# Attention with rotary embedding and an MLP on one core: the first four weight chunks move from GpSimd's DMA queue to SyncE's, and the planner's load rate and due times are new

## The chip, the core and the metric

The kernel runs on one core of a Trainium2 chip. The metric is the device time of one execution in microseconds; the median of several runs stands for a kernel. Five engines work side by side, each through its own list of instructions in order: TensorE (PE in the profile), VectorE (DVE), ScalarE (ACT), GpSimd (POOL) and SyncE (SP). Here SP and POOL hardly compute; they issue DMAs. What SP issues goes to one DMA queue (q1 in the profile), what POOL issues to another (q0), and 16 DMA engines serve both.

## The reference

Inputs are float32. There are 4 batches, 8 heads, 576 positions, 64 columns a head; the MLP is 512 to 2048 to 512 over all 2304 tokens.

```python
q_rot, k_rot = (rotate(q), rotate(k))            # [x1 cos - x2 sin, x1 sin + x2 cos]
scores = np.matmul(q_rot, k_rot.transpose(0, 1, 3, 2)) / np.sqrt(D)
attn = np.exp(scores - np.max(scores, axis=-1, keepdims=True))
attn = attn / (np.sum(attn, axis=-1, keepdims=True) + 1e-09)
x = np.matmul(attn, v)      # heads put side by side: 2304 x 512
h = x @ w_in
g = np.where(h >= 1, h, np.where(h <= -1, 0.0, (h + 1) ** 2 / 4))
out = g @ w_out
```

The rounding of the reference is kept by splitting each float32 operand into two float16 parts and adding three products of them (hi hi, hi lo, lo hi).

## The kernel before

**Data.** Heads are worked in four pairs j. For each batch and pair the host has laid out two copies of keys and queries, transposed: the plain one, and one with the halves of each head exchanged. A rotation (`turn`, L325) is then three products on DVE: first copy times cosines (L328), second copy times sines (L330), their sum (L332). The cosines and sines are the table `rt`. Queries come in two blocks of 256 columns (`hf` 0 and 1) and 64 left-over columns (`rqL`). For batch 0 every pair of block 0 has loads of its own (keys 288 KB a copy, queries 128 KB a copy), later ones are merged.

**Splits.** `prep_k`, `load_q`, `prep_left` and `load_v` issue the loads of keys, queries, left-over columns and values. A factor from the sum of squares of the keys (ACT square L292, a small matmul L298, four small DVE steps) scales the split of keys and queries into high part (ACT L339) and low part (DVE L341).

**Attention.** `softmax_item` (L535) takes scores of a pair of heads for 128 rows: maximum on DVE (L543), exponent on ACT (L545), high part on ACT (L553), low part on DVE (L555). A DMA transpose on SP's queue (`dmaT`, L287) turns them into `pT`, and PE multiplies them with the values (L598).

**Weights.** There are 16 chunks of 1 MB, w_in and w_out by turns, i = 2c + which. `prep_w` (L481) loads one into a buffer that is free at that time: in the order `rawseq` the last regions of the weight store itself, then the value buffer `rv` and the second key buffer `kT[1]`. Chunks 0 to 3 go into four different regions, chunks 4 to 7 into the same four again, once the earlier ones are decoded. Chunk 14 goes into `kT[1]`, which nobody holds at the start. Decoding is three DVE steps (L493, L495, L497), then the high part on ACT (L506). For the first ten chunks the low part comes from PE: a product with the identity and one with a scaled diagonal (L522, L523) into the two banks `psO`, read by ACT (L526). The MLP (`mlp_block`, L661) uses the same banks `psO` for its second layer (L709), after those; its first layer is L679.

**The order.** Nothing runs in the order of the program text. Every step is given to `Plan.add` with an engine, a cost in ns, a place `at` and what it reads and writes. `wanted()` (L104) lays PE's steps one behind the other by `at`, from 18,000 ns on, and works a due time back from each step's users: minus its own cost and a lag, which for a DMA is 1300 ns and its bytes at the load rate (`bw`). `order()` (L123) adds a number from the table SLACK, by the group's name and by the name with its part ("raw k0.02 sp": loads of keys, batch 0, pair 2, on SP), and then runs through time: an engine that is free takes, of the steps that are ready, the one with the lowest sum. In this run a load moves over one shared wire at the load rate. What comes out is one list for each engine, which the chip then executes in that order, with waits only for what a step reads and writes.

Of the kernel before, what the change touches and what calls it, by code (L numbers as in the profile page):

```python
# [13 lines left out]
U32 = mybir.dt.uint32  # L14
# [8 lines left out]


SLACK = {
    "k0 dve": 41_100, "k0.00 dve": 46_400, "k1 act": 617_700, "k1 dve": 63_800, "k1.10 dve": 21_800,
    "k1.12 dve": 13_200, "k1.20 act": 39_400, "k1.20 dve": -4_900, "k1.30 dve": 385_800, "left0 act": -440_200,
    "left0 dve": -34_700, "left0.01 dve": 29_800, "left1 act": -682_100, "left1.20 dve": 4_500,
    "left1.22 dve": -1_000, "left1.32 pe": 57_700, "mlp0 act": -48_700, "mlp0 dve": -56_400, "mlp0 pe": 1_362_600,
    "mlp0.0.1 act": 186_100, "mlp0.0.2 act": 74_000, "mlp0.0.7 act": -87_400, "mlp1 dve": -637_500,  # L30
    "mlp1.1.2 act": -106_800, "mlp1.1.3 act": -122_000, "mlp2 act": -875_300, "mlp2 dve": 47_700,
    "mlp2 pe": 40_700, "mlp2.2.2 act": 1_200, "mlp2.2.3 pe": 45_800, "mlp2.2.4 dve": 63_100, "mlp3 act": -691_900,
    "mlp3 dve": -81_700, "mlp3 pe": -23_800, "mlp3.3.3 pe": 241_700, "mlp3.3.4 pe": 225_400,
    "mlp3.3.7 act": 43_400, "mlp3.3.7 pe": 162_900, "mlp3.4.2 pe": -800, "mlp3.5.1 pe": 65_600,
    "mlp3.5.2 dve": -202_300, "mlp3.5.2 pe": 29_400, "mlp3.5.7 pe": 34_500, "mlp3.6.1 pe": 20_600,
    "mlp3.6.2 pe": 25_500, "mlp3.6.7 pe": 163_600, "mlp3.7.0 pe": 82_200, "mlp3.7.3 pe": -15_800,
    "pv0 dve": -448_200, "pv0 pe": -769_100, "pv1 act": -1_444_600, "pv1 dve": -252_200, "pv1.123 pe": 71_100,
    "pv1.302 pe": -66_700, "q0 act": 100_000, "q0 dve": -18_900, "q0.001 act": -77_800, "q0.003 dve": 48_700,
    "q0.010 dve": 109_300, "q0.012 dve": 36_700, "q1 dve": 44_500, "q1.100 dve": -20_700, "q1.110 dve": 8_500,
    "q1.200 dve": -37_600, "q1.210 act": 52_900, "ql0 dve": -134_800, "ql1 dve": 190_900, "raw k0 sp": -12_600,  # L40
    "raw k0.00 sp": -14_800, "raw k0.01 sp": -368_000, "raw k0.02 sp": -12_000, "raw k0.03 sp": 11_100,
    "raw k1 sp": -1_486_700, "raw q0 sp": -6_000, "raw q0.000 sp": -9_500, "raw q0.002 sp": 50_400,
    "raw q0.003 sp": 221_800, "raw v0.0 sp": 71_700, "raw w.1 pool": -67_500, "s0 act": -70_500,
    "s0 dve": -190_500, "s0.001 dve": -66_100, "s0.003 dve": -18_000, "s0.021 dve": 65_100, "s0.022 act": 55_200,
    "s0.022 sp": 21_200, "s0.023 act": 27_000, "s0.031 act": -118_200, "s1 dve": -166_700, "s1 pe": -550_500,
    "s1.101 act": -14_300, "s1.102 act": -34_500, "s1.110 dve": -25_600, "s1.111 dve": -17_400,
    "s1.112 dve": -6_800, "s1.121 dve": 40_400, "s1.122 act": -77_600, "s1.123 act": -123_500,
    "s1.123 dve": 215_800, "s1.132 act": -109_900, "s1.201 dve": -42_600, "s1.202 dve": -25_800,
    "s1.202 sp": 14_100, "s1.210 dve": -33_500, "s1.221 dve": 5_400, "s1.223 act": -71_400, "s1.232 act": -5_500,
    "s1.233 dve": 35_700, "s1.301 dve": -5_700, "s1.302 act": -166_600, "s1.303 dve": -11_800,  # L50
    "s1.312 sp": -17_900, "s1.320 dve": -4_400, "scale0.01 dve": 99_100, "v0 act": 59_900, "v0 dve": 80_400,
    "v1 act": -52_700, "v1.2 act": 119_900, "w act": -90_000, "w dve": 37_800, "w.5 dve": 7_600,
}


# [128 lines left out]
def kernel(  # L184
# [73 lines left out]
    plan = Plan()  # L258
    counts = {}

    def ring(name, n):
        c = counts.get(name, 0)
        counts[name] = c + 1
        return c % n
# [4 lines left out]
    def act_cost(n, psum=False, ptrs=1):  # L269
        return (51.0 if psum else 93.0) + 0.833 * n + 93.0 * ptrs  # L270

    def dve_cost(n, psum=False, ptrs=0):
        return (65.0 if psum else 69.0) + 1.042 * n + 61.0 * ptrs
# [6 lines left out]

    def dma(at, dst, src, r, w, nbytes, eng="sp"):
        q = nc.sync if eng == "sp" else nc.gpsimd
        plan.add(eng, 600.0 if eng == "sp" else 1000.0, at, lambda: q.dma_start(out=dst, in_=src), r, w, bw=nbytes / 300.0)

    def dmaT(at, dst, src, r, w, nbytes):
        plan.add("sp", nbytes / 221.0 + 60.0, at,
# [2 lines left out]
    def add_square(at, x, lo, np_, scr, scrkeys, col, colkey, srckeys):  # L289
        n = x.shape[-1]  # L290
        plan.add("act", act_cost(n), at,
                 lambda: nc.scalar.activation(out=scr[lo:lo + np_, 0:n], in_=x, func=AF.Square, accum_out=col),  # L292
                 r=srckeys, w=[colkey] + scrkeys)
# [187 lines left out]
    def prep_w(which, c, at):  # L481

        yi, i = ring("ybufs", 2), 2 * c + which
        (raw, rk_), y, yk = rawseq[i], ybufs[yi], ykeys[yi]
        plan.group, plan.part = "raw w", c
        dma(at, raw, (w_out if which else w_in).bitcast(U32)[c], [], rk_, 128 * 8192, "pool")
        plan.group = "w"
        words = raw.rearrange("p (n t) -> p n t", t=2)
        lw, hw = words[:, :, 0], words[:, :, 1]
        u = y.bitcast(U32)  # L490
        hi, lo = [ws[:, i, l] for l in range(2)]

        plan.add("dve", 602.0, at, lambda: nc.vector.tensor_scalar(  # L493
            out=u, in0=hw, scalar1=3, scalar2=0x3FFFFFFF, op0=ALU.logical_shift_left, op1=ALU.bitwise_and), r=rk_, w=yk)
        plan.add("dve", 1135.0, at, lambda: nc.vector.scalar_tensor_tensor(  # L495
            out=u, in0=lw, scalar=29, in1=u, op0=ALU.logical_shift_right, op1=ALU.bitwise_or), r=rk_ + yk, w=yk)
        plan.add("dve", 1135.0, at, lambda: nc.vector.scalar_tensor_tensor(  # L497
            out=u, in0=hw, scalar=0xC0000000, in1=u, op0=ALU.bitwise_and, op1=ALU.bitwise_or), r=rk_ + yk, w=yk)
        if c == 0:
            cols = [3 * which, 3 * which + 1]  # L500
            for e, j in enumerate(cols):
                add_square(at, y[:, 512 * e:512 * e + 512], 0, 128, r_s, ["r"], ssw[:, j:j + 1], ("ssw", j), yk)
            p, ri = root(at, ssw[:, 3 * which:3 * which + 3], [("ssw", 3 * which + j) for j in range(3)])
            wcol[which] = (times(at, p, 2.0 ** 64), times(at, ri, 2.0 ** (10 - 64)))
# [241 lines left out]
    at = 0.0  # L746
# [126 lines left out]
```

## Time and profile before

| | us |
|---|---|
| runs before, median of 3 (lowest, highest) | 635.91 (634.6, 638.42) |
| the profiled execution | 636.13 |
| its span in the trace | 634.4 |
| PE, DVE, ACT busy in the span | 559.6, 510.6, 441.5 |

A busy time is the time in which an engine had an instruction under way. It is best read by stretches, since the limit changes: the start with loads and preparation, a long middle part with attention of the batches beside the MLP of earlier blocks, and an end with the MLP alone. Matmuls are pipelined, so a busy PE is not PE at its peak. DMA issues are shown under SPq, and under POOL, at the time of their issue; how long data takes is read from the queues.

### The profile page before, as it was taken

To read this page: it belongs to the slowest core of one execution; us is meant where nothing else is said; L and a number is where in the kernel's file an instruction comes from. 1 tells how busy PE (TensorE), PEld (TensorE's weight loads), DVE (VectorE), ACT (ScalarE), POOL (GpSimd) and SP (SyncE) were. 2 spreads that over 40 slices of the span, in tenths; PEclk is the share of its full clock that TensorE was granted. 3 is DMA by queue.
4 is the path that set the end of the run, shared out by engine and by line. 5 is a ranking of instruction groups with operands and counts; after the bars stand their busy time and mean duration, and the time that the engine had idled before them with its cause. 6 is when DMAs were issued, how large, how long until landed. Compare 5 with 4: busy or idle time off the path is not lost.

```text
span 634.4 us, 12628 instructions
## 1 busy us (share of the span) xinstructions
PE 559.6 (88%) x5078; PEld 358.7 (57%) x5078; DVE 510.6 (80%) x839; ACT 441.5 (70%) x881; POOL 9.3 (1%) x22
## 2 busy tenths in 40 slices
PE   0146657999889899999999999999999999999996
PEld 0023223566565666665666666666666667666663
DVE  1999989999999899999899789968877684334332
ACT  1478768997989789998777799766777574223221
POOL 2000100000000000000000000000000000000000
PEclk9999788999999999999999999999999999999999
DMA  8997797828699968686668675666464664000000
GB/s 335 389 299 146 260 253 203 179 74 178 136 184 249 211 137 199 122 212 141 119 160 177 106 146 115 100 91 107 91 140 75 117 128 90 1 1 35 1 34 17
DMA packets 188009, 91.31 MB, mean 144 GB/s; under 512 B 170160, under 2 KB 178608, under 8 KB 185904
## 3 DMA queue, kind: packets, MB, share of 16 engines
q1 hardware_dynamic: 185648, 73.74, 55.7%
q0 software_dynamic: 2304, 16.78, 7.4%
q8 instruction: 39, 0.64, 0.4%
q14 instruction: 18, 0.15, 0.1%
HBM read 40.96 MB, written 4.72 MB: 72 GB/s over the span
## 4 chain that ended last, share of the span: by engine, by line
PE 54%; DVE 24%; DMA 11%; ACT 6%; issue 3%; SPq 0%; ACTq 0%; DVEq 0%
PE psO L709 20%; PE psH L679 20%; DMA pT<-phl 9%; PE psV L598 6%; DVE phl L555 5%; PE psS L569 5%; DVE mx L543 4%; ACT phl L553 2%; DMA rk<-in_km_dram 2%; ACT p L545 1%; PE psO L522 1%; DVE g L700 1%; PE psS L581 1%; DVE r L696 1%; DVE dup L330 1%
## 5 line engine op out<-in xcount | busy, mean ns | idle before, releaser
L709 PE MATMUL psO<-w,g 128*128 128x512 f16 x864 | 211.2, 380 | 1.2 <-ACT g L698 0.9
L679 PEld LDWEIGHTS <-w 128*128 128x128 f16 x1920 | 171.2, 98 | 48.2 <-issue 6.2
L679 PE MATMUL psH<-xT,w 128*128 128x256 f16 x1536 | 188.8, 273 | 3.2 <-ACT a L686 2.2
L555 DVE SCALAR_TENSOR_TENSOR phl<-p,sums,phl 128x576 f16<-128x576 f32 x144 | 113.4, 812 | 18.1 <-ACT phl L553 17.6
L553 ACT ACTIVATE phl<-p,sums 128x576 f16<-128x576 f32 x144 | 106.7, 766 | 30.6 <-DMA pT<-phl 17.3
L545 ACT ACTIVATE p<-psS,mx 128x576 f32<-128x576 f32 x144 | 105.4, 733 | 29.1 <-DVE mx L543 25.8
L709 PEld LDWEIGHTS <-g 128*128 128x128 f16 x864 | 78.8, 98 | 75.8 <-issue 3.2
L543 DVE TENSOR_REDUCE mx<-psS 128x1 f32<-128x576 f32 x144 | 103.8, 748 | 3.5 <-PE psS L569 2.2
L700 DVE SCALAR_TENSOR_TENSOR g<-r,g 128x512 f16<-128x512 f32 x72 | 49.4, 686 | 52.6 <-ACT g L698 51.5
L569 PE MATMUL psS<-kT,qT 64*128 64x512 f16 (+1 forms) x768 | 68.1, 300 | 19.5 <-ACT p L545 17.4
L686 ACT ACTIVATE a<-psH 128x512 f32<-128x512 f32 x72 | 42.4, 589 | 60.5 <-PE psH L679 60.1
L569 PEld LDWEIGHTS <-qT 64*128 64x128 f16 x768 | 32.5, 97 | 64.8 <-issue 43.4
L698 ACT ACTIVATE g<-r 128x512 f16<-128x512 f32 x72 | 44.9, 623 | 28.1 <-PE psO L709 17.1
L598 PE MATMUL psV<-pT,vS 128*64 128x256 f16 (+1 forms) x768 | 49.5, 251 | 4.1 <-DMA pT<-phl 4.1
L696 DVE SCALAR_TENSOR_TENSOR r<-a,r 128x512 f32<-128x512 f32 x72 | 49.5, 687 | 0.9
L689 DVE SCALAR_TENSOR_TENSOR r<-a 128x512 f32<-128x512 f32 x48 | 33.1, 689 | 19.7 <-ACT a L686 18.8
L598 PEld LDWEIGHTS <-vS 128*64 128x64 f16 x768 | 33.0, 111 | 16.0 <-issue 14.2
L298 PE MATMUL psV<-ssk,ones 128*128 128x1 f32 (+1 forms) x14 | 3.4, 314 | 29.3 <-ACT w L292 28.9
L598 PE MATMUL psV<-pT,vM 128*64 128x256 f16 (+1 forms) x480 | 28.5, 249 | 0.0
L545 ACT ACTIVATION_READ_ACCUMULATOR p<-psS,mx 128x1 f32 x144 | 28.0, 194 | 0.0
L679 PE MATMUL psH<-xL,w 128*128 128x128 f16 x384 | 26.2, 219 | 0.0
L598 PEld LDWEIGHTS <-vM 128*64 128x64 f16 x480 | 21.9, 112 | 0.1
(98 smaller groups left out, 476.7 us busy)
## 6 DMA issues: line engine op xcount, KB each, us to landing
w<-in_w_in_dram POOLq DMA_DIRECT2D x7, 1024.0 KB, 7.5
w<-in_w_out_dram POOLq DMA_DIRECT2D x6, 1024.0 KB, 7.9
rv<-in_vm_dram SPq DMA_DIRECT2D x8, 512.0 KB, 6.2
out_dram<-o SPq DMA_DIRECT2D x16, 256.0 KB, 2.4
rq<-in_qm_dram SPq DMA_DIRECT2D x7, 512.0 KB, 5.0
dup<-in_qm_dram SPq DMA_DIRECT2D x7, 512.0 KB, 4.0
rk<-in_km_dram SPq DMA_DIRECT2D x6, 576.0 KB, 5.1
dup<-in_km_dram SPq DMA_DIRECT2D x6, 576.0 KB, 5.4
```

What stands on the lines that cost most here:

```text
L543: plan.add("dve", dve_cost(S, psum=True), at, lambda m=m, src=src: nc.vector.tensor_reduce(out=m, in_=src, op=ALU.max, axis=AX.X, negate=T ...
L545: plan.add("act", act_cost(S, psum=True, ptrs=2), at, lambda a=a, e=e, m=m, src=src: nc.scalar.activation(out=p32[e], in_=src, func=AF.Exp ...
L553: plan.add("act", act_cost(S), at, lambda a=a, e=e, hi=hi: nc.scalar.activation(out=hi, in_=p32[e], func=AF.Copy, scale=rr[:, a:a + 1]), r ...
L555: plan.add("dve", dve_cost(S, ptrs=1), at, lambda a=a, e=e, hi=hi, lo=lo: nc.vector.scalar_tensor_tensor(out=lo, in0=p32[e], scalar=rr[:, ...
L569: nc.tensor.matmul(out=psS[a][:, lo:hi], lhsT=qT[hf][d, l, j, c:c + 128], rhs=kT[ks][d, j, m, lo:hi], start=z == 0, stop=z == 2)
L598: nc.tensor.matmul(out=outs[a], lhsT=st, rhs=moving(a, blk), start=z == 0, stop=z == len(seq) - 1)
L679: nc.tensor.matmul(out=psH[:, n * i:n * i + n], lhsT=wi[ft // 2][:, wl, kk, 128 * (ft % 2):128 * (ft % 2) + 128], rhs=xfn(xl, kk), start=z ...
L686: plan.add("act", act_cost(512, psum=True, ptrs=0), at, lambda one=one: nc.scalar.activation(out=a, in_=psH, func=AF.Relu, scale=2.0 ** -7 ...
L696: plan.add("dve", dve_cost(512), at, lambda one=one: nc.vector.scalar_tensor_tensor(out=r, in0=a, scalar=one, in1=r, op0=ALU.max, op1=ALU. ...
L698: plan.add("act", act_cost(512, ptrs=0), at, lambda g=g, one=one: nc.scalar.activation(out=g[:, 0], in_=r, func=AF.Relu, scale=1.0, bias=- ...
L700: plan.add("dve", dve_cost(512), at, lambda g=g, one=one: nc.vector.scalar_tensor_tensor(out=g[:, 1], in0=r, scalar=-one, in1=g[:, 0], op0 ...
L709: nc.tensor.matmul(out=psO[pos[tt]], lhsT=g[:, gl, n * i + 128 * tt:n * i + 128 * tt + 128], rhs=wo[ft // 2][:, wl, ft % 2, :], start=ft = ...
```

## The change

Three places change. Weight chunks 0 to 3 are issued by SP instead of POOL. The load rate of the planner's wire, which also enters the due times, is 400 instead of 300 bytes per ns. The table SLACK is another one throughout. Costs, buffers, arithmetic, RAMP and the planner's code stay. The lines of SLACK that the text speaks of:

```diff
 SLACK = {
-    "k0 dve": 41_100, "k0.00 dve": 46_400, "k1 act": 617_700, "k1 dve": 63_800, "k1.10 dve": 21_800,
...
-    "q1.200 dve": -37_600, "q1.210 act": 52_900, "ql0 dve": -134_800, "ql1 dve": 190_900, "raw k0 sp": -12_600,
-    "raw k0.00 sp": -14_800, "raw k0.01 sp": -368_000, "raw k0.02 sp": -12_000, "raw k0.03 sp": 11_100,
-    "raw k1 sp": -1_486_700, "raw q0 sp": -6_000, "raw q0.000 sp": -9_500, "raw q0.002 sp": 50_400,
-    "raw q0.003 sp": 221_800, "raw v0.0 sp": 71_700, "raw w.1 pool": -67_500, "s0 act": -70_500,
...
-    "v1 act": -52_700, "v1.2 act": 119_900, "w act": -90_000, "w dve": 37_800, "w.5 dve": 7_600,
+    "k0 act": 511_600, "k0.01 act": 40_000, "k0.02 dve": -171_800, "k1 act": 679_600, "k1 dve": 49_500,
...
+    "ql1.1 act": 46_800, "raw k0 sp": -6_200, "raw k0.00 sp": -31_100, "raw k0.02 sp": -19_900,
+    "raw k0.03 sp": 6_600, "raw q0 sp": -622_100, "raw q0.010 sp": 72_700, "raw v0 sp": 52_400,
+    "raw w sp": -5_500, "s0 act": 41_000, "s0 dve": -281_100, "s0 pe": -26_300, "s0.010 dve": -3_300,
...
+    "v1 act": 1_258_200, "v1 dve": -1_199_000, "w dve": 111_300, "w pe": -47_900, "w.4 dve": -45_500,
 }
...
     def dma(at, dst, src, r, w, nbytes, eng="sp"):
         q = nc.sync if eng == "sp" else nc.gpsimd
-        plan.add(eng, 600.0 if eng == "sp" else 1000.0, at, lambda: q.dma_start(out=dst, in_=src), r, w, bw=nbytes / 300.0)
+        plan.add(eng, 600.0 if eng == "sp" else 1000.0, at, lambda: q.dma_start(out=dst, in_=src), r, w, bw=nbytes / 400.0)
...
         plan.group, plan.part = "raw w", c
-        dma(at, raw, (w_out if which else w_in).bitcast(U32)[c], [], rk_, 128 * 8192, "pool")
+        dma(at, raw, (w_out if which else w_in).bitcast(U32)[c], [], rk_, 128 * 8192, "sp" if i < 4 else "pool")
```

## Rows read from the trace of the kernel before

**Rows 1.** Page: busy us (share of span) and instructions of each engine.

```profile
PE 559.6 (88%) x5078; PEld 358.7 (57%) x5078; DVE 510.6 (80%) x839; ACT 441.5 (70%) x881; POOL 9.3 (1%) x22
```

**Rows 2.** Stretches: from:to, length, busy us of each engine, clock, DMA share, GB/s.

```profile
0.00:15.30 15.30, 0.00 (x0) 0.00 (x0) 2.21 (x9) 2.06 (x3) 3.45 (x11) 1.00 0.88 334
15.30:110.00 94.70, 51.78 (x292) 24.70 (x294) 92.17 (x173) 70.71 (x141) 4.66 (x9) 0.91 0.90 259
110.00:300.00 190.00, 180.48 (x1646) 116.79 (x1644) 185.68 (x283) 171.31 (x343) 1.14 (x3) 1.00 0.78 169
300.00:600.00 300.00, 298.87 (x2875) 199.01 (x2872) 220.21 (x362) 190.00 (x384) 0.00 (x0) 1.00 0.51 96
```

**Rows 3.** Timeline 0 to 40: start, us, engine, line, operation [idle before, releaser].

```profile
10.03 0.76 DVE L330 TENSOR_TENSOR w<-w,rt 128x576 f32<-128x576 f32 x1 [7.44 <-DMA w<-in_km_dram]
...
13.23 1.28 ACT L292 ACT_TABLE_LOAD   x1 [13.23 <-DMA rk<-in_km_dram]
...
15.33 0.76 DVE L328 TENSOR_TENSOR rk<-rk,rt 128x576 f32<-128x576 f32 x1 [4.54 <-ACT w L292]
...
24.43 0.69 DVE L493 TENSOR_SCALAR o<-w 128x1024 uint32<-128x1024 uint32 x1
...
29.37 0.42 DVE L328 TENSOR_TENSOR rq<-rq,rt 128x256 f32<-128x256 f32 x1
...
31.78 1.62 PE L569 MATMUL psS<-kT,qT 64*128 64x512 f16 x12 [0.19 <-ACT qT L339]
```

**Rows 4.** Timeline 0 to 40, DMA issues of SP, and POOL's fifth (into kT).

```profile
0.74 0.40 SPq L283 DMA_DIRECT2D rt<-in_rot_dram  x1
...
1.20 0.42 SPq L283 DMA_DIRECT2D rk<-in_km_dram  x1
...
1.66 0.43 SPq L283 DMA_DIRECT2D w<-in_km_dram  x1
...
2.13 0.92 SPq L283 DMA_DIRECT2D rk<-in_km_dram  x2
...
3.09 1.03 SPq L283 DMA_DIRECT2D w<-in_km_dram  x2
...
3.65 0.53 POOL L283 DMA_DIRECT2D kT<-in_w_in_dram  x1
4.17 0.96 SPq L283 DMA_DIRECT2D rq<-in_qm_dram  x1
...
5.66 0.44 SPq L283 DMA_DIRECT2D rk<-in_km_dram  x1
9.95 0.33 SPq L283 DMA_DIRECT2D rq<-in_qm_dram  x1
...
13.17 0.33 SPq L283 DMA_DIRECT2D w<-in_qm_dram  x1
```

**Rows 5.** DMA queues, 0 to 5 us, then 5 to 10: packets, MB, share.

```profile
q1 hardware_dynamic: 316, 0.95, 57.3%
q0 software_dynamic: 6, 0.05, 4.6%
...
q0 software_dynamic: 188, 1.41, 73.4%
q1 hardware_dynamic: 210, 0.44, 23.6%
```

**Rows 6.** Stretch 60 to 100 us, columns as in rows 2.

```profile
60.00:100.00 40.00, 27.11 (x169) 12.25 (x168) 37.93 (x51) 31.05 (x55) 3.17 (x6) 0.83 0.92 250
```

**Rows 7.** Chain of waits: start, us, what; and landing of all transposes (L287).

```profile
79.41 17.32 DMA pT<-phl x2
...
DMA to landing us min/median/max: 3.2/5.1/11.1
```

**Rows 8.** Lines L522 and L709: duration ns min/median/max, first and last start.

```profile
L522 PE MATMUL psO<-o,xL x20: 590/592/1193, 59.5 to 123.0; 128*128 128x512 f32 x20
...
L709 PE MATMUL psO<-w,g x864: 376/379/390, 126.2 to 629.1; 128*128 128x512 f16 x173
```

More of the change, by code (lines that the diff above doesn't have):

```diff
@@ L25 @@
 SLACK = {
-    "k0 dve": 41_100, "k0.00 dve": 46_400, "k1 act": 617_700, "k1 dve": 63_800, "k1.10 dve": 21_800,
[L27 to L39, printed above, removed]
-    "q1.200 dve": -37_600, "q1.210 act": 52_900, "ql0 dve": -134_800, "ql1 dve": 190_900, "raw k0 sp": -12_600,
@@ L41 @@
-    "raw k0.00 sp": -14_800, "raw k0.01 sp": -368_000, "raw k0.02 sp": -12_000, "raw k0.03 sp": 11_100,
-    "raw k1 sp": -1_486_700, "raw q0 sp": -6_000, "raw q0.000 sp": -9_500, "raw q0.002 sp": 50_400,
-    "raw q0.003 sp": 221_800, "raw v0.0 sp": 71_700, "raw w.1 pool": -67_500, "s0 act": -70_500,
-    "s0 dve": -190_500, "s0.001 dve": -66_100, "s0.003 dve": -18_000, "s0.021 dve": 65_100, "s0.022 act": 55_200,
-    "s0.022 sp": 21_200, "s0.023 act": 27_000, "s0.031 act": -118_200, "s1 dve": -166_700, "s1 pe": -550_500,
@@ L46 @@
[L46 to L50, printed above, removed]
@@ L51 @@
-    "s1.312 sp": -17_900, "s1.320 dve": -4_400, "scale0.01 dve": 99_100, "v0 act": 59_900, "v0 dve": 80_400,
-    "v1 act": -52_700, "v1.2 act": 119_900, "w act": -90_000, "w dve": 37_800, "w.5 dve": 7_600,
+    "k0 act": 511_600, "k0.01 act": 40_000, "k0.02 dve": -171_800, "k1 act": 679_600, "k1 dve": 49_500,
+    "k1.10 dve": 60_700, "k1.12 dve": 64_900, "k1.20 dve": 41_400, "k1.22 dve": 150_900, "left0 act": -12_800,
+    "left0.00 dve": 5_000, "left0.02 act": -183_900, "left0.02 dve": -15_900, "left0.02 pe": -58_300,
@@ new lines @@
+    "left1 dve": -379_800, "left1 pe": -510_800, "mlp0.0.1 act": -34_200, "mlp0.0.6 act": 43_900,
+    "mlp0.0.6 dve": -3_900, "mlp1 act": 27_800, "mlp1 dve": 54_900, "mlp1 pe": -7_900, "mlp1.1.0 pe": -7_500,
+    "mlp1.1.1 act": 49_500, "mlp1.1.3 act": 25_000, "mlp1.1.3 dve": -49_400, "mlp1.1.4 pe": -8_500,
+    "mlp1.1.5 dve": 30_300, "mlp1.1.6 dve": 21_000, "mlp2 dve": 47_400, "mlp2 pe": 147_600, "mlp2.2.0 pe": 78_600,
+    "mlp2.2.1 dve": 92_100, "mlp2.2.3 pe": 80_300, "mlp2.2.6 pe": -47_100, "mlp2.2.7 pe": -11_700,
@@ new lines @@
+    "mlp3 dve": 8_900, "mlp3 pe": -45_600, "mlp3.3.1 dve": 140_900, "mlp3.3.3 pe": 81_300, "mlp3.3.4 pe": 173_800,
+    "mlp3.3.6 dve": 37_900, "mlp3.3.7 act": 34_100, "mlp3.4.0 pe": 35_900, "mlp3.5.2 pe": -24_800,
+    "mlp3.5.5 pe": -30_600, "mlp3.5.6 pe": 98_000, "mlp3.6.2 dve": 66_000, "mlp3.6.6 pe": 48_400,
+    "mlp3.7.1 act": -20_000, "mlp3.7.1 pe": 12_100, "mlp3.7.3 pe": -3_000, "mlp3.7.4 pe": 78_800,
+    "pv0 act": 184_500, "pv1 dve": -351_600, "pv1 pe": 2_100, "pv1.202 pe": 34_500, "pv1.320 pe": 6_900,
@@ new lines @@
+    "pv1.321 pe": -44_500, "q0 act": 344_700, "q0 dve": 58_900, "q0.010 dve": -12_400, "q0.011 dve": 36_700,
+    "q0.013 dve": 50_300, "q1 act": 1_300_900, "q1 dve": 93_600, "q1.100 dve": 25_800, "q1.110 dve": 43_700,
+    "q1.300 dve": 91_500, "q1.310 dve": 47_600, "ql0 act": 814_800, "ql0 dve": 19_500, "ql1 dve": 51_800,
+    "ql1.1 act": 46_800, "raw k0 sp": -6_200, "raw k0.00 sp": -31_100, "raw k0.02 sp": -19_900,
+    "raw k0.03 sp": 6_600, "raw q0 sp": -622_100, "raw q0.010 sp": 72_700, "raw v0 sp": 52_400,
@@ new lines @@
+    "raw w sp": -5_500, "s0 act": 41_000, "s0 dve": -281_100, "s0 pe": -26_300, "s0.010 dve": -3_300,
+    "s0.011 pe": 69_400, "s0.012 dve": -24_600, "s0.020 dve": -24_400, "s0.021 act": -24_100, "s0.022 pe": 76_100,
+    "s0.023 dve": 40_200, "s1 act": 84_100, "s1 dve": 6_000, "s1 pe": -489_100, "s1.101 act": -8_500,
+    "s1.103 act": 85_500, "s1.103 dve": 53_200, "s1.110 act": 38_700, "s1.112 dve": -2_800,
+    "s1.121 dve": -120_300, "s1.122 dve": -64_700, "s1.132 act": 152_800, "s1.200 act": 56_200,
@@ new lines @@
+    "s1.202 act": -75_200, "s1.202 dve": 176_900, "s1.211 dve": -11_700, "s1.231 dve": -12_600,
+    "s1.232 dve": 103_200, "s1.233 dve": -86_400, "s1.301 dve": 20_400, "s1.321 dve": -13_300,
+    "scale0 dve": 5_400, "scale0.00 dve": 83_400, "scale0.02 dve": -28_700, "scale1 dve": -32_700,
+    "scale1.10 pe": 86_000, "scale1.20 dve": 64_700, "v0 act": 323_700, "v0 dve": -28_900, "v0.0 act": 34_900,
+    "v1 act": 1_258_200, "v1 dve": -1_199_000, "w dve": 111_300, "w pe": -47_900, "w.4 dve": -45_500,
```

## The prediction

> **What bounds the kernel now.** I read the page's busy times first, then the same in stretches, then the order of instructions in the first 32 us, then the DMA queues of that stretch, and last the chain of waits.
>
> The page gives PE 559.6 us of a span of 634.4 [rows 1], so 74.8 us without matmuls is all that a better order can win. The stretches say where it lies [rows 2]: PE is idle for 15.3 us up to 15.3, for 94.7 - 51.8 = 42.9 us up to 110, for 9.5 us from 110 to 300, and for 1.1 us from 300 to 600. So PE is the bound from 300 on. From 15.3 to 110 it is DVE: 92.2 of 94.7 us busy while PE runs half of the time, and from 110 to 300 both are nearly full (185.7 and 180.5 of 190). Until 15.3 nobody is: DVE worked 2.2 us. Time is to be had there: 13.1 us in which the engine that limits the next 95 us has no data.
>
> Why it has none is in the first instructions [rows 3]. DVE's first real work, a key product, starts at 10.03 after waiting for its DMA; the first ACT square of a key waits for another until 13.23; DVE is steady only from 15.33, and the first scores run on PE at 31.78. The loads themselves [rows 4]: SP issues ten loads by 5.66 and then one at 9.95 and one at 13.17: from there each seems to wait for an older one to land (10.03 and 13.23 are the times at which DVE and ACT get theirs). Beside them POOL has issued its fifth weight load, of 1.05 MB like the others, at 3.65. The queue counts of 5 to 10 us [rows 5] show who is served: POOL's queue moves 1.41 MB in 188 packets, SP's 0.44 MB in 210. The packets alternate about one to one and a weight packet is far larger, so the keys get 24% of the wire while weights get the rest. The second decode of those weights begins only at 24.43 [rows 3], so most of what held the keys up was not yet wanted.
>
> **The change part by part.** It has three edits: four of POOL's first loads go to SP, the planner's load rate is 400 instead of 300 bytes per ns, and the table SLACK is new throughout.
>
> *The order on SP.* The diff shows no order; it follows from wanted() (a due time worked back from PE's order) plus SLACK, lowest first among what is ready. Worked by hand for the kernel before, in thousands: first copy of key j=1 about -360, of j=0 -13, of j=2 -10; second copy of j=0 0, of j=2 10; first query pair and first copy of key j=3 both near 13.6; and that is the order of SP's rows [rows 4]. The same arithmetic for the kernel after: all queries of batch 0 lie near -590 to -510 ("raw q0" is -622.1), first copies of keys 0 and 2 at -23 and -11, second copy of 0 at -10, weight chunks 0 and 1 at 5 and 7, second copy of key 2 and first copy of 1 at 9, chunks 2 and 3 at 9 and 12, the other keys at 16 to 39, the values last at 85. So I expect queries, two keys, then weights among the rest, and not weights behind everything. The last chunk (drawn into kT) keeps POOL's queue; it is then POOL's first load.
>
> *Issue cost.* SP issues four more loads. SP's issues here take 0.4 to 1.0 us [rows 4], so 1.6 to 4 us of SP, at a time when it waits for landings anyway: 0. If that cover goes, the first transposes wait behind the values, which come last; I bound this at 0 to 4 us of delay for one transposed block.
>
> *When data lands.* By 5.0 us SP's queue had moved 0.95 MB and POOL's almost nothing [rows 5]: POOL's data begins there. Table of angles 0.59 MB and first query pair 0.26 MB make 0.85 MB: an estimate of 5.5 us for DVE's first turn, with 0.5 us for the landing. POOL's one chunk then takes 1.05 / (1.41 / 5) = 3.7 us, to 8.7 us, in which SP gets 0.09 MB per us; after it SP has the wire, 0.37 MB per us (1.41 + 0.44 in 5 us). The last query pair is there at about 10 us, the last columns and second query block at 13.5, key 0's first copy at 14.3, its second at 16, weight chunk 0 at 19.
>
> *What DVE does with it.* A turn is three products, 0.42 us each for a query pair [rows 3]: four pairs are 5.0 us; the last columns (as wide) are 1.25, and the second query block, four times as wide, about 3.7. That is 10 us of work on DVE that needs no key, between 5.5 and 16 us, where the kernel before does 0.76. Then keys and weights are there. I take 1.5 us off for gaps while POOL's chunk is on the wire, and 1 us for the changeover to keys: 15.3 - 5.5 - 0.8 - 2.5 = 6.5 us of DVE work earlier. Bounds: 0, if an instruction that waits for a key stands in DVE's order ahead of the queries (the key is not earlier than before: 14.3 and 16 us against 13.23 and 15.33), and 10 us if there is no gap.
>
> *What the end sees of it.* DVE has only 2.5 us of idle time from 15.3 to 110, so work brought forward there moves everything behind it, and the first scores, which in the kernel before stand behind two weight decodes, come as early as 20 us. From 110 on PE takes over; its queue of work starts that much earlier. So I pass on 6.5 us whole. By the same reading every us that DVE stands still between 16 and 110 us costs one.
>
> *The rest of the table.* Every step of all four batches may move. From 300 to 600 us PE has 1.1 us of idle time: nothing to win there, only to lose. Between 60 and 100 us PE idles 40 - 27.1 = 12.9 us [rows 6], and the chain of waits names two DMA transposes in it that took 17.3 us, where the median of a landing is 5.1 [rows 7]: POOL's later weight loads are on the wire then. A new order may meet or miss such a collision. Neither side has a reason here: 0, with bounds of -7 (a little over half of the 12 us too many) and +7.
>
> Sum: the profiled execution took 636.13 us, 1.7 over its span and 0.2 over the median of the three runs, 635.91. 636.1 - 6.5 = 629.6 for it, 629.4 against the median.
>
> **The rivals.** *The gain is absorbed.* The same bytes cross the same wire: in the window from 5 to 10 us both queues together moved 1.85 MB, and all of batch 0's inputs with five chunks are about 11.7 MB, 32 us in either order. If DVE, having done the queries, stands still for the keys behind 2.4 MB of queries, or if PE's and DVE's nearly full stretch from 110 to 300 us needs what comes later (chunks 4 on, which POOL loads when a region is free), the end is where it was: 636, within 2 us. The Trainium skill has a rule on this side: DMA: Bandwidth & Descriptors, section "Issuing engines are not separate DMA queues", says that loads of several engines run on the same 16 DMA engines, and that issuing from more of them saves only issue time. By that rule alone, moving four issues would be worth nothing here and the time 636. The rows speak against that reading, since the queue decides who waits: 24% and 76%.
>
> *The collision goes too.* If the new order also parts weight loads and transposes between 80 and 97 us, 6.5 + 7 = 13.5 us: 622. For it: a planner whose loads last as long as they do; against: the eight later chunks still come from POOL in the same stretch.
>
> *Slower: the MLP starts late.* Ten chunks are split with the help of PE into the two PSUM banks of the MLP's sums, and in program order before it: the last of those products is at 123.0 and the MLP's first second-layer product at 126.2 [rows 8]. The SLACK of the weights on DVE rises from 37.8 to 111.3 thousand, so decoding yields more often to keys, queries and values. While the MLP is out, PE has too little: 12.9 of 40 us idle [rows 6], 0.32 us per us. From 20 us later than 126 on (146) the 6.5 us are spent; at 160 the time is 636 - 6.5 + 0.32 x 34 = 640. Against it: a decode deferred gives DVE softmax work that PE needs too, and DVE's total is the same.
>
> *It does not do what it says.* If weights are really behind keys and values (my ranks wrong), first copies of keys land by 6 to 8 us, weights at 20 to 30: DVE starts at the same time with keys in place of queries: 629 as well.
>
> **How the numbers follow.** Forecast (with the last case) 0.47; collision gone as well 0.15; absorbed 0.22; slower 0.16. The likeliest gives 629.4. Its own range is 624 to 633 (10 us and 3 us brought forward). To leave out no more than 2 in 10 the range reaches half a case further on both sides: 621 (622 and 1 more) to 641 (the MLP at 160). About 0.5%, 3.2 us, is what a measurement of this kernel can tell from no change; faster is 0.47 + 0.15 = 0.62, same 0.22, slower 0.16.
>
> **What would show it.** In the profile after: DVE's first product at 5 to 7 us and on query tiles, DVE's busy time up to 15.3 us at 8 to 9 us instead of 2.2; the first scores at 20 to 25 us; POOL's queue moving only 1 MB before 20 us; PE's idle time up to 110 us about 6 us less than 58, and from 110 on as before. Wrong would be: DVE waiting for keys until 14 us or later, the first second-layer product of the MLP later than 126, or PE idle between 300 and 600 us.

## The result and the profile after

The changed kernel is slower: 638.69 us (17 runs, 636.68 to 646.96) against 634.1 (17 runs, 631.24 to 638.63) for the kernel before beside it, a ratio of 1.0065 with a 95% interval of 1.0046 to 1.0084. The run of 646.96 fell in a slower state that the ratio leaves out; without it the highest is 639.48. The forecast was 629.4, with a range of 621 to 641: the time lies inside the range, but on the other side of the kernel before. The profiled execution took 638.67 us with a span of 635.7. The two traces lie closer together (636.13 and 638.67 us, spans 634.4 and 635.7) than the medians, so they show 1.3 to 2.5 of the 4.6 us. Lines of the code stand one further down than before (L283 is now L284); in the kernels of the experiments a few more.

The page after, busy times as in [rows 1]:

```profile
PE 558.5 (88%) x5078; PEld 360.3 (57%) x5078; DVE 510.6 (80%) x839; ACT 439.5 (69%) x881; POOL 7.3 (1%) x18
```

The work is the same to a tenth of a microsecond on DVE; the difference is idle time. Where it lies, by the stretches of the kernel after (columns as in [rows 2]):

```profile
0.00:15.30 15.30, 0.00 (x0) 0.00 (x0) 7.04 (x22) 0.00 (x0) 1.37 (x7) 1.00 0.82 276
15.30:110.00 94.70, 49.63 (x295) 27.23 (x296) 84.35 (x156) 67.91 (x137) 4.30 (x8) 0.91 0.94 271
110.00:300.00 190.00, 180.56 (x1714) 116.56 (x1714) 188.75 (x289) 174.12 (x351) 1.59 (x3) 1.00 0.76 170
300.00:600.00 300.00, 298.27 (x2788) 197.20 (x2787) 219.34 (x359) 189.42 (x382) 0.00 (x0) 1.00 0.51 95
```

Against [rows 2], DVE wins 7.04 - 2.21 = 4.8 us up to 15.3, and loses 92.17 - 84.35 = 7.8 from there to 110. Taken together it is 3.0 us behind at 110, and PE 2.2 us (49.63 of 51.78). From 110 on PE's numbers are those of before. TensorE's granted clock does not differ: it is 0.91 of full speed from 15.3 to 110 us and 1.00 from there to 600 in both kernels. So the loss is made between 15.3 and 110, in DVE's 10.35 us of idle time (2.5 before).

The start came in the order that was worked out by hand, but for one copy of a key. Timeline of the kernel after, first 30 us (start, us, engine, line, operation, [idle before, releaser]):

```profile
0.74 0.40 SPq L284 DMA_DIRECT2D rt<-in_rot_dram  x1
1.20 0.42 SPq L284 DMA_DIRECT2D rq<-in_qm_dram  x1
1.43 0.67 POOL L284 DMA_DIRECT2D kT<-in_w_in_dram  x1
...
5.34 0.42 DVE L329 TENSOR_TENSOR rq<-rq,rt 128x256 f32<-128x256 f32 x1 [2.75 <-DMA rq<-in_qm_dram]
...
9.23 0.43 DVE L331 TENSOR_TENSOR w<-w,rt 128x256 f32<-128x256 f32 x1 [3.47 <-DMA w<-in_qm_dram]
...
10.64 0.62 SPq L284 DMA_DIRECT2D rk<-in_km_dram  x1
...
13.10 0.64 SPq L284 DMA_DIRECT2D w<-in_w_in_dram  x1
...
16.52 1.28 ACT L293 ACT_TABLE_LOAD   x1 [16.52 <-DMA rk<-in_km_dram]
...
21.18 2.82 SPq L284 DMA_DIRECT2D rv<-in_vm_dram  x2
...
27.42 1.62 PE L570 MATMUL psS<-kT,qT 64*128 64x512 f16 x12
```

Queries go first, then two keys with both copies (by hand the second copy of key 2 stood behind two weight chunks), then weights among the other keys, values last. DVE starts on a query at 5.34 (10.03 before, [rows 3]), but stops after its first product until 9.23: POOL's one remaining chunk is on the wire then. The queues of the kernel after from 5 to 10 us (packets, MB, share), to be held against [rows 5]:

```profile
q0 software_dynamic: 143, 1.04, 50.6%
q1 hardware_dynamic: 707, 0.65, 40.2%
```

Most of SP's packets come at the end of that stretch. In its middle, 6 to 8 us, it is:

```profile
q0 software_dynamic: 88, 0.72, 85.4%
q1 hardware_dynamic: 71, 0.07, 11.0%
```

The packets alternate about one to one, as in [rows 5], but a packet of the queries is only about 1 KB (0.07 MB in 71), so SP gets 9% of the bytes and not 24%.

The idle time after 15.3 us has names. DVE's waits from 15.3 to 110 in the kernel after (engine, tile, line, what for: us in total, times, longest):

```profile
DVE mx L544 <- PE psS L570: 5.3, 1, 5.3
DVE rk L329 <- DMA rk<-in_km_dram: 3.0, 1, 3.0
DVE rk L329 <- ACT w L293: 1.2, 1, 1.2
```

**The 3.0 us, near 57.** Timeline of the kernel after, 45 to 62 us:

```profile
47.63 0.53 POOL L284 DMA_DIRECT2D rv<-in_w_out_dram  x1 [20.94 <-DVE vS L342]
48.79 0.88 SPq L284 DMA_DIRECT2D rk<-in_km_dram  x2
...
50.14 0.53 POOL L284 DMA_DIRECT2D w<-in_w_out_dram  x1 [1.99 <-DVE qL L342]
...
60.10 1.36 DVE L329 TENSOR_TENSOR rk<-rk,rt 128x1152 f32<-128x1152 f32 x1 [2.98 <-DMA rk<-in_km_dram]
```

POOL issues chunk 13 (into `rv`) and chunk 5, 2 MB together, around SP's keys of batch 1. Those keys need 60.10 - 48.79 = 11.3 us until DVE can use them. In the kernel before the three lie far apart, and DVE does not wait. Timeline of the kernel before (load 5, the keys, DVE on them, loads 13 and 10):

```profile
29.02 0.53 POOL L283 DMA_DIRECT2D w<-in_w_out_dram  x1 [6.07 <-DVE o L497]
...
38.18 0.33 SPq L283 DMA_DIRECT2D rk<-in_km_dram  x1
...
55.59 1.35 DVE L328 TENSOR_TENSOR rk<-rk,rt 128x1152 f32<-128x1152 f32 x1
...
70.58 0.53 POOL L283 DMA_DIRECT2D rv<-in_w_out_dram  x1 [6.63 <-DVE vS L341]
...
94.29 0.53 POOL L283 DMA_DIRECT2D w<-in_w_in_dram  x1 [9.16 <-DVE sums L550]
```

**The 5.3 us, near 105.** Timeline of the kernel after, 93 to 125 us:

```profile
94.27 0.53 POOL L284 DMA_DIRECT2D w<-in_w_in_dram  x1 [6.71 <-DVE xT L498]
...
103.39 1.06 PE L599 MATMUL psV<-pT,vS 128*64 128x256 f16 x8 [6.14 <-DMA pT<-phl]
...
106.52 1.62 PE L570 MATMUL psS<-kT,qT 64*128 64x512 f16 x12
...
108.17 1.42 DVE L544 TENSOR_REDUCE mx<-psS 128x1 f32<-128x576 f32 x2 [5.33 <-PE psS L570]
```

POOL issues chunk 10 at 94.27, the same time as before (94.29), but beside other transposes. PE stands 6.14 us at a product with the values because the transposes that bring `pT` are late; the next scores stand behind that product in PE's list; DVE waits for those scores. The DMA queues of the kernel after, 92 to 96 us and then 96 to 100, show what happens to the transposes:

```profile
q1 hardware_dynamic: 2070, 0.52, 108.5%
q0 software_dynamic: 10, 0.06, 11.9%
...
q1 hardware_dynamic: 429, 0.11, 14.2%
q0 software_dynamic: 137, 1.00, 77.8%
```

While the chunk is on the wire SP's queue moves 0.11 MB in 4 us; before it, 0.52. None of these three loads was urgent: by their places in DVE's list, chunk 5 is decoded from 79 us on, chunk 10 from 121 and chunk 13 from 162.

### The profile page after: what moved, and what is told of

Same layout as the page of the kernel before. It is cut to its first block, busy times and chain, and to the rows that moved or that the text cites. A ratio compares the mean times of both kernels' runs of the same rounds, so it can differ in the third digit from the quotient of the medians.

```text
span 635.7 us, 12664 instructions
## 1 busy us (share of the span) xinstructions
PE 558.5 (88%) x5078; PEld 360.3 (57%) x5078; DVE 510.6 (80%) x839; ACT 439.5 (69%) x881; POOL 7.3 (1%) x18
## 4 chain that ended last, share of the span: by engine, by line
PE 50%; DVE 27%; DMA 12%; ACT 6%; issue 3%; SPq 1%; DVEq 0%; ACTq 0%
PE psO L710 19%; PE psH L680 19%; DVE phl L556 6%; PE psV L599 6%; DVE mx L544 5%; PE psS L570 4%; DMA pT<-phl 4%; DMA rq<-in_qm_dram 3%; DMA rv<-in_vm_dram 3%; DVE g L701 2%; DVE r L697 2%; DMA w<-in_w_out_dram 2%; ACT p L546 1%; SPq L284 1%; DVE w L515 1%
## 5 line engine op out<-in xcount | busy, mean ns | idle before, releaser
L710 PE MATMUL psO<-w,g 128*128 128x512 f16 x864 | 211.7, 379 | 2.0 <-ACT g L699 0.9
L710 PEld LDWEIGHTS <-g 128*128 128x128 f16 x864 | 79.5, 98 | 74.0 <-issue 2.2
L570 PE MATMUL psS<-kT,qT 64*128 64x512 f16 (+1 forms) x768 | 66.2, 296 | 14.7 <-ACT p L546 8.9
L570 PEld LDWEIGHTS <-qT 64*128 64x128 f16 x768 | 31.0, 97 | 60.5 <-issue 39.7
L599 PE MATMUL psV<-pT,vS 128*64 128x256 f16 (+1 forms) x768 | 51.8, 259 | 12.5 <-DMA pT<-phl 11.8
L599 PEld LDWEIGHTS <-vS 128*64 128x64 f16 x768 | 34.8, 114 | 25.5 <-issue 16.7
L599 PE MATMUL psV<-pT,vM 128*64 128x256 f16 (+1 forms) x480 | 30.1, 256 | 0.8 <-DMA vM<-vS 0.7
```

The lines of the kernel that those rows point to most:

```text
L570: nc.tensor.matmul(out=psS[a][:, lo:hi], lhsT=qT[hf][d, l, j, c:c + 128], rhs=kT[ks][d, j, m, lo:hi], start=z == 0, stop=z == 2)
L599: nc.tensor.matmul(out=outs[a], lhsT=st, rhs=moving(a, blk), start=z == 0, stop=z == len(seq) - 1)
L710: nc.tensor.matmul(out=psO[pos[tt]], lhsT=g[:, gl, n * i + 128 * tt:n * i + 128 * tt + 128], rhs=wo[ft // 2][:, wl, ft % 2, :], start=ft = ...
```

## The experiments

**Theory A**: the start is a real gain, and it is lost again because POOL's later loads now run beside batch 1's keys and beside transposes. **Theory B**: the new order is worse in itself, wherever the loads are.

The diffs of this section are shortened: they say what an edit does and leave out the lines that carry it.

**1 and 2. Later loads without weight on the wire.** In both kernels POOL's loads 4 to 13 and 15 carry a sixteenth of their columns; the plans keep the full size. That part of the weights is left out, so most of the MLP works on what the buffers held.

```diff
-        dma(at, raw, src, [], rk_, 128 * 8192, ...)
+        part = 128 if i >= 4 and i != 14 else 2048     # of 2048 columns
+        dma(at, raw[:, 0:part], src[:, 0:part], [], rk_, 128 * 8192, ...)
```

> The kernel after, in the same order, but POOL's weight loads 4 to 13 and 15 bring only a sixteenth of their bytes (the rest of those chunks is left out of the computation). Theory A: the new order does bring DVE's work forward at the start by about 5 us, and loses it again between 50 and 110 us because these loads share the wire with the keys of batch 1 and with transposes. Then the waits of DVE at 57 to 60 and at 103 to 108 us are gone, PE's first value products do not wait for transposes, and the time is 627 to 631 us. Theory B: the new order is the worse one whatever is on the wire. Then it stays within 2 us of the kernel after, 637 to 640.

> The kernel before with the same cut: weight loads 4 to 13 and 15 bring a sixteenth of their bytes (the rest is left out of the computation). Theory A: it gains less than the kernel after does by the cut, since its own collision near 90 us costs DVE 1.7 us: 630 to 633 us, and it ends later than the kernel after with the cut. Theory B: it stays 4 us ahead of the kernel after with the cut.

Measured: 630.74 us for the list of after (ratio to the kernel before 0.9925, 0.9898 to 0.9953) and 631.93 for that of before (0.9962, 0.9937 to 0.9987). The kernel before took 634.81 beside both.

Stretch 0 to 110 us of experiment 1 (columns as in [rows 2]):

```profile
0.00:110.00 110.00, 54.98 (x339) 30.14 (x340) 100.41 (x189) 76.27 (x152) 6.18 (x16) 0.95 0.72 207
```

and of experiment 2:

```profile
0.00:110.00 110.00, 54.05 (x308) 26.46 (x309) 96.02 (x184) 73.35 (x145) 8.27 (x20) 0.94 0.73 201
```

The later loads cost the new list 638.69 - 630.74 = 8.0 us and the old list 634.81 - 631.93 = 2.9. That is 5.1 us of contention more in the new list, and it speaks for A. Free of it, the new list's DVE is 4.4 us ahead at 110 us, but the time only 1.2 by the medians, 2.3 by the ratios (0.37% of 634) and 2.9 by the two profiled spans, 625.8 and 628.7. The two intervals overlap, so how much of DVE's lead reaches the end stays uncertain; all three figures are below the lead. PE, which limits from 110 us on, is only 0.9 us ahead there by its busy time (54.98 and 54.05).

**3. Edit 1 undone in the new list.** Same plan, same lists, but chunks 0 to 3 are issued by POOL again.

```diff
-        q = nc.sync if eng == "sp" else nc.gpsimd
+        q = nc.sync if eng == "sp" and not (weights and i < 4) else nc.gpsimd
```

> The kernel after with every engine's list as planned, only that weight chunks 0 to 3 are issued by POOL, where they stand behind the load into kT and start by 4 us. Theory A: queries and keys get a quarter of the wire for 20 us, DVE loses most of what it had won by 15.3 us (7.0 us of work against 2.2) and waits longer for keys: 641 to 645 us. Theory B, in which the start does not matter: 637 to 640.

Measured: 647.59 us (ratio 1.0189, 1.0154 to 1.0224), 9 us over the kernel after and more than the 641 to 645 expected. Timeline of this kernel, the first square of a key:

```profile
26.42 1.28 ACT L295 ACT_TABLE_LOAD   x1 [26.42 <-DMA rk<-in_km_dram]
```

Nearly 10 us later than the 16.52 of the kernel after, for the same keys from the same place in SP's list. Only the queue of four loads was changed. With it their time changes too: POOL issues them from 2.09 to 3.65 us, SP in the kernel after from 13.10 to 16.46, behind its queries and two keys. How much each of these two makes was not separated.

**4. Edit 1 alone in the old list.** The kernel before, planned as before, with chunks 0 to 3 taken out of the finished list and issued by SP behind the last key load of batch 0.

```diff
-        q = nc.sync if eng == "sp" else nc.gpsimd
+        q = nc.sync if eng == "sp" or (weights and i < 4) else nc.gpsimd
...
     order = plan.order()
+    (steps of loads 0 to 3 move behind the last "raw k0 sp")
```

> The kernel before with every engine's list as planned, only that weight chunks 0 to 3 are issued by SP, right behind the last key load of batch 0. Nothing is left out. The keys have the wire almost to themselves after POOL's one load, so that DVE should be steady from 9 or 10 us and not 15.3, if the weights of chunk 0 (wanted at 18 us) are there by then. Theory A, in which a start won is won as long as nothing takes it back: 629 to 632 us. Theory B, in which the start does not decide: 633 to 636.

Measured: 635.09 us (ratio 0.9996, 0.9973 to 1.002), no gain, against the expectation. Timeline of this kernel, 0 to 20 us:

```profile
9.34 0.76 DVE L332 TENSOR_TENSOR w<-w,rt 128x576 f32<-128x576 f32 x1 [6.75 <-DMA w<-in_km_dram]
...
19.10 0.69 DVE L496 TENSOR_SCALAR xT<-w 128x1024 uint32<-128x1024 uint32 x1 [3.21 <-DMA w<-in_w_in_dram]
```

The keys are there 0.7 us earlier (9.34; 10.03 in [rows 3]) and DVE is busy for 4.7 us up to 15.3. But the list of before has a weight decode next, chunk 0 now comes behind all keys, and DVE waits 3.2 us for it at the head of its list: what is brought forward by one load is waited for at another.

**5 and 6. Shorter loads.** Each POOL load as four of 256 KB, so that the transposes and keys might get in between.

```diff
-        q.dma_start(out=dst, in_=src)
+        for p in range(4):                             # POOL only
+            q.dma_start(out=dst[:, p * m:(p + 1) * m], in_=src[:, p * m:(p + 1) * m])
```

> The kernel before with each POOL load of a weight chunk issued as four loads of a quarter of the columns, so that its packets are a quarter as large; lists and bytes stay. Theory A, in which large packets of POOL's queue push keys and transposes aside: SP's share beside POOL rises from 24% to about half, DVE is steady from 10 to 12 us and not 15.3, transposes are held up less, 629 to 632 us. If the packet's size does not matter: 634 to 636.

> The kernel after with the same quarters for POOL's loads; lists and bytes stay. Theory A: keys of batch 1 land before 58 us, the transposes near 94 us end by 100, 632 to 635 us. If the packet's size does not matter: 637 to 640.

Measured: 652.13 us with the list of before (ratio 1.027, 1.0225 to 1.0315) and 651.74 with that of after (1.0263, 1.0232 to 1.0295). Both are far from what was expected. Part of the aim was met in experiment 5 (queues, 5 to 10 us):

```profile
q0 software_dynamic: 277, 0.94, 63.6%
q1 hardware_dynamic: 332, 0.68, 37.0%
```

SP's keys get 42% of the bytes instead of 24% [rows 5]. POOL's packets are not a quarter as large, but a little under half: 16.78 MB in 5120 packets over the whole run against 2304 before. But POOL could no longer issue ahead. Timeline of experiment 5, POOL:

```profile
1.44 2.27 POOL L289 DMA_DIRECT2D w<-in_w_in_dram  x4
3.70 2.12 POOL L289 DMA_DIRECT2D w<-in_w_out_dram  x4
8.45 0.54 POOL L289 DMA_DIRECT2D w<-in_w_in_dram  x1 [2.63 <-DMA w<-in_w_in_dram]
```

After eight loads POOL waits for the first to land before it issues the ninth. The transposes did not land sooner either: from 80 to 100 us their median is 12.1 us (9.7 before) in experiment 5, and the wire moves 221 GB/s there (263 before). From 110 to 300 us PE has 174.17 us of work in experiment 5, 180.48 before [rows 2]. Of the 12.7 us between the two spans (647.1 and 634.4) PE's idle time makes 6.9 and its busy time 5.8 (565.4 against 559.6, at a mean granted clock of 0.972 against 0.985). Those 20 us hold other steps in the two kernels, so the lower rate need not come from the quarters. Why fewer bytes move there, and what part of the 17 us each of these makes, is not settled.

**7 and 8. Which later load costs what.** As experiment 1, but only loads 5 and 13 are cut, or only load 10.

```diff
-        part = 128 if i >= 4 and i != 14 else 2048
+        part = 128 if i in (5, 13) else 2048           # 7; in 8: i in (10,)
```

> The kernel after, only POOL's loads 5 and 13 (issued at 47.6 and 50.1 us) bring a sixteenth of their bytes (the rest of these two chunks is left out of the computation). If the loss sits where DVE waits for the keys of batch 1: that wait (3.0 us, and 1 us ahead of it) is gone and the time is 634 to 636. If the loss is spread over all collisions: 637 to 639.

> The kernel after, only POOL's load 10 (issued at 94.3 us, beside the transposes for which PE waits 6.1 us and DVE behind it 5.3 us) brings a sixteenth of its bytes (the rest of that chunk is left out of the computation). If the loss sits there: those two waits shrink to 1 or 2 us and the time is 633 to 636. If it is spread: 637 to 639.

Measured: 635.21 us (ratio 1.0004, 0.9985 to 1.0022) and 633.43 (0.9986, 0.997 to 1.0003). Against the 638.69 of the kernel after that is 3.5 and 5.3 us, close to the waits that each removes (3.0 and 5.3), and 8.8 together, close to the 8.0 of all eleven loads. By the ratios, which compare each kernel with the runs beside it, it is 3.9, 5.0 and 8.9 for all eleven; each figure is good to one or two us. In each of the two the wait in question is gone from DVE's list of waits. As far as this scatter lets one see, three loads out of eleven hold the whole loss.

**9 and 10. The same loads later, nothing left out.** In the finished list of after, load 5 goes to SP's queue at its place (behind the keys and queries of batch 1), load 10 to SP's queue behind a query copy that SP issues near 100 us, and load 13 stays on POOL behind load 12. Experiment 10 also issues load 14 (the one into `kT`, on the wire from 5 to 10 us) behind load 11.

```diff
+        q = nc.sync if eng == "sp" or (weights and i in (5, 10)) else nc.gpsimd
...
     order = plan.order()
+    behind(wload[13], wload[12])
+    behind(wload[10], tq)              # tq: second copy of a query block, batch 1
+    behind(wload[14], wload[11])       # experiment 10 only
```

> The kernel after, complete, with three of the later weight loads moved and every other step where it was: load 5 goes through SP's queue at its place, right behind the loads of batch 1's keys and queries; load 10, whose decode comes only near 121 us, goes through SP's queue behind the transposes issued by 100.5 us; load 13, used near 164 us, is issued by POOL behind load 12. If the two collisions are the loss (they were 3.5 and 5.3 us when their bytes were left out), the same comes back with all bytes moved: 629 to 632 us, faster than both kernels. If moved loads only collide elsewhere: 634 to 638.

> The run before with one more load moved: load 14 (into kT, used near 150 us), POOL's first, is issued behind load 11. Then nothing shares the wire with the queries and keys at the start, DVE has done 9 to 10 us of work by 15.3 us and not 7. If work of DVE won at the start reaches the end whole, as the prediction had it: 2 to 3 us below the run before. If PE is not waiting for that work: within 1 us of it.

Measured: 634.03 us (ratio 0.9986, 0.9968 to 1.0004) and 631.56 (0.9952, 0.9924 to 0.998). Experiment 9 gets 4.7 of the 8 us back, less than expected (629 to 632); PE still waits 5.2 us for transposes up to 110. Experiment 10 is 2.8 us faster than the kernel before beside it, by medians 7.1 below the kernel after, and the fastest of the complete kernels here. Stretches of experiment 10:

```profile
0.00:15.30 15.30, 0.00 (x0) 0.00 (x0) 8.79 (x25) 0.44 (x1) 0.70 (x6) 1.00 0.82 272
...
0.00:110.00 110.00, 55.80 (x328) 30.09 (x329) 99.66 (x188) 75.01 (x148) 4.54 (x13) 0.94 0.90 271
```

and the same of experiment 9:

```profile
0.00:15.30 15.30, 0.00 (x0) 0.00 (x0) 7.13 (x22) 0.00 (x0) 1.37 (x7) 1.00 0.81 278
...
0.00:110.00 110.00, 52.84 (x319) 28.80 (x320) 97.47 (x185) 73.11 (x145) 4.55 (x13) 0.94 0.91 271
```

One load of 1 MB out of the first 10 us gives DVE 1.7 us there, 2.2 at 110, and the end 2.5 by the medians (the two intervals overlap a little). The wait for the first query's second copy shrinks from 3.47 to 0.51 us. Timeline of experiment 10, 0 to 20 us:

```profile
6.20 0.43 DVE L333 TENSOR_TENSOR w<-w,rt 128x256 f32<-128x256 f32 x1 [0.51 <-DMA w<-in_qm_dram]
```

**11 and 12. The other edits.** Experiment 11 is the kernel before with edit 1 alone, planned anew with the old SLACK and the old rate. Experiment 12 is the kernel after with the old rate.

```diff
+    "raw w.1 sp": -67_500, "raw w.1 pool": -67_500,                 # 11, SLACK of the kernel before
+        dma(at, raw, ..., 128 * 8192, "sp" if i < 4 else "pool")    # 11
...
-        ..., bw=nbytes / 400.0)
+        ..., bw=nbytes / 300.0)                                     # 12, in the kernel after
```

> One edit alone: the kernel before with weight chunks 0 to 3 planned and issued on SP, its own SLACK and the load rate of 300. Chunks 0 and 1 then stand behind the first key's pair, ahead of the other keys. If the queue alone helps: 629 to 632 us. If an order must be made for it: 634 to 642, since keys 0 and 2 wait for 2 MB in the same queue.

> One edit undone: the kernel after planned with the load rate of 300. The order on SP stays the same in the first 30 us; later loads and transposes are planned apart by other amounts. If the rate of 400 makes the planner believe that loads and transposes fit where they collide, 300 gives a better or equal time: 634 to 639 us. If the new SLACK only fits the rate of 400: above 640.

Measured: 652.17 us (ratio 1.0273, 1.0244 to 1.0301) and 652.15 (1.0277, 1.0236 to 1.0317). Experiment 11 is 10 us over the upper end of what was expected. Two weight chunks stand ahead of keys 0 and 2 on SP, issued at 2.13 and 2.61 us. They are chunks 2 and 3, and not 0 and 1 as the expectation has it: the old table's -67,500 for "raw w.1" moved to SP with them. Chunks 0 and 1, decoded first, are issued at 12.69 and 15.18. Timeline of this kernel:

```profile
18.10 0.76 DVE L328 TENSOR_TENSOR rk<-rk,rt 128x576 f32<-128x576 f32 x1 [7.04 <-ACT w L292]
```

The old table was made for a list on SP without weights in it; how much of the loss this one entry makes was not tried. Experiment 12 starts like the kernel after (DVE 7.80 us up to 15.3), but falls behind later. Stretch 110 to 300 us of experiment 12:

```profile
110.00:300.00 190.00, 175.72 (x1600) 112.76 (x1598) 183.97 (x281) 167.96 (x340) 1.59 (x3) 0.97 0.76 170
```

PE has 4.8 us less there than in the kernel after. With some of the three edits and not the others (experiments 3, 4, 11 and 12) the time lies between that of the kernel before and 18 us more. Where the lists were planned anew (11 and 12), a table fits only the queue and the rate that it stands beside. Which due times go wrong in experiment 12 wasn't followed.

**All of them in one table** (medians; DVE and PE are busy us up to 110 of the profiled execution):

| kernel | us | DVE to 110 | PE to 110 | PE 110 to 300 |
|---|---|---|---|---|
| before | 634.1 to 634.8 | 94.38 | 51.78 | 180.48 |
| after | 638.69 | 91.39 | 49.63 | 180.56 |
| 1 after, loads small | 630.74 | 100.41 | 54.98 | 182.84 |
| 2 before, loads small | 631.93 | 96.02 | 54.05 | 183.58 |
| 3 after, weights on POOL | 647.59 | 87.36 | 43.94 | 177.82 |
| 4 before, weights on SP | 635.09 | 94.38 | 53.31 | 184.51 |
| 5 before, quarters | 652.13 | 88.76 | 50.98 | 174.17 |
| 6 after, quarters | 651.74 | 90.18 | 46.65 | 172.06 |
| 7 after, 5 and 13 small | 635.21 | 94.78 | 51.96 | 182.08 |
| 8 after, 10 small | 633.43 | 95.97 | 51.11 | 182.58 |
| 9 after, loads later | 634.03 | 97.47 | 52.84 | 181.34 |
| 10 as 9, load 14 too | 631.56 | 99.66 | 55.80 | 182.03 |
| 11 before, edit 1, replanned | 652.17 | 90.26 | 48.64 | 173.09 |
| 12 after, old rate | 652.15 | 93.04 | 48.16 | 175.72 |

In the kernels with the list of after and whole loads on POOL's side (after, 1, 3, 7 to 10) time falls as DVE's work up to 110 us grows, but for the 0.6 us between 8 and 9: from 91.4 to 100.4 us of work it falls by 8.0, 0.9 us for each. Experiment 3 lies off that line: it has 4.0 us of work less than the kernel after and takes 8.9 us more. Quarters and replanned lists do not lie on that line: they lose more after 110.

## Why the prediction was wrong

**What bounds it** held for this change: the stretches up to 110 us decide, the time goes with DVE's work in them, and from 300 on PE has nothing to lose (298.27 of 300).

**The order on SP** held: queries, keys 0 and 2, weights among the other keys, values last. The rival "it doesn't do what it says" falls with it.

**DVE's start** was right in its place and too large in its size. DVE began on queries at 5.34 (5.5 expected), but did 7.04 us up to 15.3 and not 8 to 9: 4.8 us earlier instead of 6.5. I took 1.5 us off for POOL's chunk, and the wait for it was 3.47. The 0.09 MB per us that SP was to get beside it came from rows of keys; the queries with their smaller packets got 0.07 MB in 2 us. Experiment 10, which moves that chunk, gives 8.79. The first scores came at 27.42, not at 20 to 25, and PE was idle for 60.4 us up to 110 where 6 less than 58 were forecast.

**The queue has a price, as assumed.** In experiment 3 the same loads in the same lists cost 9 us more from POOL's queue, from which they also go out 11 to 13 us earlier. The prediction set its rows against the rule of the Trainium skill, DMA: Bandwidth & Descriptors, section "Issuing engines are not separate DMA queues". By that rule it would have been nothing. In [rows 5] 188 packets stand beside 210, and 88 beside 71 from 6 to 8 us of the kernel after. The Trainium skill, DMA: Bandwidth & Descriptors, section "Queues, rings and completion order", says that each DMA engine goes round its queues packet by packet. These counts agree with that. From 96 to 100 us, 137 packets of POOL stand beside 429 of the transposes, which agrees less well.

**"I pass on 6.5 us whole"** is the first step that failed. It rested on DVE's 2.5 us of idle time between 15.3 and 110, which was a property of the old order and not of the engine. In the new order DVE met keys that had not landed and scores that stood behind late transposes, and it stood 10.35 us. The sentence beside it, that every us that DVE stands still there costs one, held for the lists from the kernel after on: 0.9 in the table, 3.5 and 5.3 us for waits of 3.0 and 5.3. Yet without the later loads 4.4 us of DVE's lead were worth only 1.2 to 2.9 us at the end, and PE's lead at 110 was 0.9. So DVE's lead did not become one of PE there. Between experiments 9 and 10 it did: 2.2 us of DVE's work at 110 went with 3.0 of PE's and 2.5 at the end. Why not in the first case isn't settled.

**"The rest of the table: 0, with bounds of -7 and +7"** is the term that was mis-sized. The collision was seen and priced (12 us too many in one place), but put at zero because no reason spoke for a side. There was one, to be had from the lists alone: POOL issues a later load when its region is free and not when it is wanted, and the new table moves both the regions' release and the keys. Load 5 goes out at 50.14 instead of 29.02, since DVE ends the decode of chunk 1 at 49.9 instead of 28.7; load 13 at 47.63 instead of 70.58; the keys of batch 1 at 48.79 instead of 38.18. It is not the lead of the start that makes them meet: DVE comes to those keys at 57.1, where its wait begins, 1.5 us later than before. It cost 8.0 us where the old order paid 2.9. By medians: 634.8 - 1.2 (the start) + 8.0 - 2.9 = 638.7. This sum comes out by construction, since its terms are differences of the same four times; it shows the sizes and is no test. What tests them is experiments 7 to 10.

**A sum and a reading.** A start of 10 us brought forward is 626 from 636, not the 624 at which the prediction's own range begins. And the 12 us too many of [rows 7] set two transposes (17.3 us) against one median landing; against two it is 7.1. Taking all eleven later loads off the wire was worth only 2.9 us to the old order.

**The rivals.** "The collision goes too" had the right mechanism and the wrong sign. "The gain is absorbed" named DVE standing still for keys, which is a part of it: 1.2 us at the first square and 3.0 at batch 1, and 3.47 for queries before that. "The MLP starts late" isn't it. Lines L523 and L710 of the kernel after (duration ns min/median/max, first and last start):

```profile
L523 PE MATMUL psO<-o,xL x20: 590/592/697, 59.7 to 124.3; 128*128 128x512 f32 x20
...
L710 PE MATMUL psO<-w,g x864: 376/379/390, 128.6 to 630.7; 128*128 128x512 f16 x173
```

The MLP's second layer begins at 128.6, 2.4 us later than in [rows 8]. So one of the signs of being wrong did show, but the point from which that rival decides was 146. The slower outcome came from a mechanism that had no case of its own on that side: transposes and batch 1's keys behind weight loads.

## What to carry to other kernels

An engine with no idle time in a stretch is fed by the order as it is; before passing on a gain whole, ask which loads its next steps need and what else is on the wire when they are wanted. A large load that nobody waits for yet is not free: here three of them cost 8.8 us, and issuing these and one more later, or behind the small loads on their queue, gave 7.1 us with nothing left out. A table of due times belongs to the queues and rates it was made for: in the two cases where one of them was changed and the lists were planned anew under the same table, the time rose by 18 us over the kernel before.

## What the runs showed of the hardware

- In two stretches POOL's and SP's queue alternated about one to one by packets, not by bytes: 188 packets beside 210 (1.41 and 0.44 MB, 5 to 10 us before), 88 beside 71 (0.72 and 0.07 MB, 6 to 8 us after). The queue with small packets got little of the wire. Beside transposes it was not one to one (137 and 429).
- A 1 MB load on POOL's queue almost stops the DMA transposes on SP's: 429 packets in 4 us against 2070 in the 4 us before, in the kernel after.
- Four loads of 256 KB in place of one of 1 MB gave the other queue a larger share at the start (42% against 24%), at packets of a little under half the size.
- POOL issued eight loads ahead, and the ninth waited for the first to land (8.45 us in experiment 5). SP issued ten by 6.1 us before, and the next at 9.95 [rows 4].
